# Attention's steps beside a feed-forward: from slots to a count of matmuls

## The chip, the cores and the metric

The kernel runs on one core of a Trainium2 chip. The metric is the device time of one execution in microseconds (us). TensorE multiplies matrices into PSUM (eight banks), VectorE and ScalarE work element by element and read PSUM, GpSimd (POOL) works element by element on SBUF only, and SyncE (SP) issues most of the DMA transfers.

## The reference

Three layers follow each other. The first is attention with sink and window, on q, k, v of 2 batches, 8 heads, 768 positions and 64 channels:

```python
keep = is_sink | in_window            # 4 sink keys, window of 128
scores = np.where(keep, scale * q @ k.T, -1e9)
a = np.exp(scores - scores.max(-1)); a = a / (a.sum(-1) + 1e-09)
x = a @ v                             # as 1536 tokens x 512
```

The second is a feed-forward: `g = relu(x @ w_in) ** 2`, `y = g @ w_out`, with 512 x 2048 and 2048 x 512 weights. The third is another one of the same size on y, whose activation is a rational function of `y @ w_in`. Weights come as 64-bit floats and are converted on the chip.

## The kernel before, in words

The 1536 tokens are cut into three groups of 512. The first feed-forward runs group by group (`group(g)`, L763), each in 16 blocks f of 128 hidden channels. A block has a first product (`gemm1`, L456: four parts of three matmuls into one PSUM bank; each operand is held as a high and a low part, hence three), an activation (`act1`, L471: three ScalarE and one VectorE instruction) and, two blocks later, a second product (`gemm2a`, L482: four times two matmuls on the high part, then four on the low part). So a block is 12 + 8 + 4 = 24 matmuls of 512 columns. The last two second products of a group come after its blocks, together with the split of the next group's x into high and low parts (`split_x`, L412). In group 0 the weights are loaded and converted as well (`wconv`, L635); in group 2 those of the third layer are.

Attention is cut into 24 units of two heads and 256 queries, eight for each group. The eight of group 0 run in a prologue. The other sixteen run beside groups 0 and 1, one group ahead of their use, as generators (`att_unit`, L373). A unit goes through these steps, one for each `next`: scores on TensorE into two banks, with maximum on VectorE (L203) and exponential on ScalarE (L209); the sums, their reciprocal and the scaling (VectorE and POOL, L214 to L220); nothing; the load of its values; the transposes on TensorE (L226) with one copy on ScalarE and one on VectorE (L231); the product with the values on TensorE (L245) and a ScalarE copy of the result into `x32` (L393); and a last step that only ends it. All these steps share PSUM banks 6 and 7.

`tick` (L583) does one step of every unit that is under way, and every third tick begins a new unit. So ticks carry scores, transposes and values in turn. The ticks are emitted with raised priority. In groups 0 and 1 the order of TensorE is the order of the program; on the other engines a scheduler with a cost model sets it. When ticks are called is decided by `slot` (L783), which is called three times in a block, after the first product and its activation, between the two halves of the second product, and at the block's end:

```python
nt = PER * NUNIT[g] + PER                      # 27 ticks in a group
def slot(k):
    nonlocal pos
    first = 9 if g == 0 else -2
    while pos < min(nt, nt * (k - first) // (3 * NF - first - 2)):
        tick()
        pos += 1
```

After a group's blocks, a loop calls further ticks until the units of the next group are done (L822).

Of the kernel before, what the change touches and what calls it, by code (L numbers as in the profile page):

```python
# [27 lines left out]
NF = DFF // P  # L28
# [9 lines left out]
NORM_POOL = (0,)  # L38
YEVAC_ACT = (0, 1)
PINNED = (0, 1)  # L40
NUNIT = (8, 8)
NCONV = 7
SCB = ((2, 3), (6, 7))
PER = 3
# [3 lines left out]
LAG = 2  # L48
# [207 lines left out]
class Fast:  # L256
# [116 lines left out]
    def att_unit(self, u, raws, alt):  # L373

        x = Unit(self, u, raws, alt)
        x.scores([self.att_bank() for _ in range(2)])
        for i, k in x.blocks:
            x.maximum(i, k)
            x.exponential(i, k)
        yield  # L380
        x.sum()
        for i, k in x.blocks:
            x.scale(i, k)
        for _ in range(ST_T):
            yield
        x.vv = self.att_load_v(u, 0)
        yield
        for k in range(2):
            x.transpose(k, self.att_bank())
            x.copy(k)  # L390
        yield
        x.values(self.att_bank())
        self.nc.scalar.copy(self.x32[u[0]][:, u[1], x.xs], x.ob[:, : x.n])  # L393
        yield

    def fill(self, b, n):
        z = self.zero.unsqueeze(1).to_broadcast([P, 4, P])
# [58 lines left out]
    def gemm1(self, which, f, xhi, xlo, n):  # L456
        h = self.h_bank()
        for c in range(NC):
            self.gemm1_part(which, f, c, (xhi, xlo), n, h)
        return h  # L460

    def gemm1_part(self, which, f, c, x, n, h):
        nc = self.nc
# [15 lines left out]
        nc.vector.tensor_tensor(glo, r, ghi.bitcast(F32), op=ALU.subtract)  # L479
        return ghi, glo  # L480

    def gemm2a(self, f, gg, n, acc, between):  # L482
        nc = self.nc
        ghi, glo = gg
        whi, wlo = self.w[(0, f, 1)]
        for m in range(NC):
            ms = slice(m * P, (m + 1) * P)
            nc.tensor.matmul(acc[m], whi[:, ms], ghi, start=(f == 0), stop=False)  # L488
            nc.tensor.matmul(acc[m], wlo[:, ms], ghi, start=False, stop=False)  # L489
        if between:  # L490
            between()
        for m in range(NC):
            ms = slice(m * P, (m + 1) * P)
            nc.tensor.matmul(acc[m], whi[:, ms], glo, start=False, stop=(f == NF - 1))  # L494


    def act2(self, h):
# [32 lines left out]
    def run(self, ctx):  # L530
# [46 lines left out]
        n0 = sum(1 for u in us if u[0] == 0)  # L577
        done = 0
# [4 lines left out]
        def tick():  # L583
            with ExitStack() as c:
                if urgent:
                    c.enter_context(tc.high_priority(offset=HP))
                tick_()
            self.va_hist.append((self.lastV, self.lastA))

        def tick_():  # L590
            nonlocal done, tick_no, ui
            if tick_no % PER == 0 and loaded:
                u, raws = loaded.pop(0)
                g = u[0]
                if g not in self.x32 and g > 0:
                    self.new_x32(g)
                a = self.att_unit(u, raws, 0)
                ui += 1
                next(a)
                new = True  # L600
            else:
                new = False
            for b in list(active)[::-1]:
                if next(b, "end") == "end":
                    active.remove(b)
                    done += 1
            if new:
                active.append(a)
                if not loaded:
                    prefetch()  # L610
            tick_no += 1
# [60 lines left out]
        with tc.manual_schedule(engines={E.Activation, E.DVE}):  # L672
# [43 lines left out]
            done = n0  # L716
# [4 lines left out]
        urgent = True  # L721
        acc, gs, ys, ysp = None, {}, {}, {}

        def second(which, g, f, between=None):
            nonlocal acc
            if f == 0:
                acc = [self.bank(k)[:, : GN[g] if which == 0 else 512] for k in range(4)]
            gg = gs.pop((which, g, f))
            if which == 0:
                n = GN[g]  # L730
                self.gemm2a(f, gg, n, acc, between)
                if f == NF - 1:
                    k = 0 if g == NG - 1 else g
                    y = self.yp.tile([P, self.yw[k]], F32, tag=f"y{k}", name="y")
                    y = y[:, : NC * n].rearrange("p (m n) -> p m n", m=NC)
                    for m in range(NC):
                        (A.copy if m % 2 == 0 or g in YEVAC_ACT else V.tensor_copy)(y[:, m], acc[m])
                    ys[g] = y
            else:
                self.gemm2b(f, gg, acc)  # L740
                if f == NF - 1:
                    for t in range(TG2 // P):
                        if g == NT2 - 1:
                            if t == 0:
                                ot = self.xp.tile([P, 4, DM], F32, tag="xhi", name="ot")
                            o = ot[:, t]
                        else:
                            o = self.stage.tile([P, DM], F32, tag="wt", name="o", bufs=2)
                        r0 = g * TG2 + t * P
                        dst = self.io["out"][r0 : r0 + P, :]  # L750
                        if g == NT2 - 1 and t == TG2 // P - 1:
                            A.copy(o[:, : DM // 2], acc[t][:, : DM // 2])
                            nc.scalar.dma_start(dst[:, : DM // 2], o[:, : DM // 2])
                            V.tensor_copy(o[:, DM // 2 :], acc[t][:, DM // 2 :])
                            nc.sync.dma_start(dst[:, DM // 2 :], o[:, DM // 2 :])
                        else:
                            (A.copy if t % 2 == 0 else V.tensor_copy)(o, acc[t])
                            nc.sync.dma_start(dst, o)

        gdone = [sum(1 for u in us if u[0] <= g) for g in range(NG)]  # L760
        sp, pos, nt = None, 0, 0

        def group(g):  # L763
            nonlocal sp, acc, pos, nt
            n = GN[g]
            last = g == NG - 1
            if last:
                assert done == len(us)
                sa.close()
                sp = ExitStack()  # L770
                self.ysp = mk(sp, "ysp", 1, "right")
                self.cp = self.ysp
                self.yx = self.yp.tile([P, self.yw[2]], F32, tag="y2", name="yx")
                self.flag()
                self.coefficients()
                wload(1, 3)
                nt = 0
            else:
                nt = PER * NUNIT[g] + PER
            self.att_banks = [6, 7]  # L780
            pos = 0

            def slot(k):  # L783
                nonlocal pos
                first = 9 if g == 0 else -2
                while pos < min(nt, nt * (k - first) // (3 * NF - first - 2)):
                    tick()
                    pos += 1

            for f in range(NF):  # L790
                if (g, f) == (0, 12):
                    self.hint((mybir.EngineType.SP, self.lastD))
                if g == 0 and f < HEAD:
                    h = hb[f]
                elif g == 0 and f == HEAD:
                    h = self.bank(6)
                    for c in range(NC):
                        self.gemm1_part(0, f, c, self.x[0], n, h)
                else:
                    h = self.gemm1(0, f, *self.x[g], n)  # L800
                gs[(0, g, f)] = self.act1(h, n)
                if g == 0 and f + 4 < NF:
                    wconv(0, f + 4, 0)
                if last and f > 0:
                    wconv(1, f - 1, 0)
                slot(3 * f + 1)
                if f >= LAG:
                    second(0, g, f - LAG, lambda: slot(3 * f + 2))
                else:
                    slot(3 * f + 2)  # L810
                if g == 0 and f + 1 < NF:
                    wconv(0, f + 1, 1)
                if last:
                    if f >= 3:
                        wconv(1, f - 3, 1)
                    if f in (4, 6, 8, 10):
                        with ExitStack() as cc:
                            cc.enter_context(tc.issue_after(self.lastX.ins))
                            self.split_y(0, (f - 4) // 2, ys, ysp)
                slot(3 * f + 3)  # L820
            if not last:
                while done < gdone[g + 1]:  # L822
                    tick()
                self.new_x(g + 1)
                for c in range(NC):
                    self.split_x(g + 1, c)
            else:
                wconv(1, NF - 1, 0)
            for f in range(NF - LAG, NF):
                second(0, g, f)  # L830
# [265 lines left out]
```

## Time and profile before

| | us |
|---|---|
| median of 3 runs | 633.92 (631.86 to 634.03) |
| profiled execution | 631.83 |
| its span, first to last instruction | 630.0 |
| TensorE busy | 609.5 (97%) |
| VectorE busy | 416.7 (66%) |
| ScalarE busy | 407.1 (65%) |
| GpSimd busy | 116.8 (19%) |
| mean granted TensorE clock | 0.995 |

Group 0's blocks begin at about 48 us, group 1's at about 160, group 2's at 273, the third layer's at about 365. In the rows PE is TensorE, DVE is VectorE, ACT is ScalarE. A matmul's end is modelled, so of two matmuls in a row the shown durations overlap; the distance between their starts is the time that one takes. A row that merges several instructions has their number after the x.

### The profile page before, as it was taken

How to read it: one execution, taken by the hardware profiler on the slowest of the kernel's cores; microseconds unless marked ns; L12 is line 12 of the kernel's file. 1: busy time of each engine (PE TensorE's matmuls, PEld its weight loads, DVE VectorE, ACT ScalarE, POOL GpSimd, SP SyncE). 2: the span in 40 equal slices, each digit the busy share in tenths (PEclk: the TensorE clock that was granted, in tenths of full speed). 3: DMA queues.
4: the chain of work that ended last, by engine and by line, in shares of the span. 5: the costliest groups of instructions: out<-in, count | busy, mean ns of one | idle time of the engine just before them, and what ended most of it. 6: DMA issues, size and time to landing. Idle time of an engine off the chain costs nothing.

```text
span 630.0 us, 9425 instructions
## 1 busy us (share of the span) xinstructions
PE 609.5 (97%) x3465; PEld 485.9 (77%) x3465; DVE 416.7 (66%) x832; ACT 407.1 (65%) x838; POOL 116.8 (19%) x119
## 2 busy tenths in 40 slices
PE   7889999999899999999999999999999999999996
PEld 3557777777677778888888888888888888888885
DVE  5987777454342232155666469988999897877783
ACT  4878988665554353276777567766686676766663
POOL 2220101010010000030000013234354332222221
PEclk9999999999999999999999999999999999999999
DMA  8846686434121200005555300000010000100002
GB/s 293 298 145 206 215 273 211 163 110 150 56 73 54 82 29 1 2 34 165 181 191 199 134 1 0 2 0 1 2 55 12 0 2 1 68 0 1 0 2 70
DMA packets 19347, 54.80 MB, mean 87 GB/s; under 512 B 2528, under 2 KB 3808, under 8 KB 19296
## 3 DMA queue, kind: packets, MB, share of 16 engines
q1 hardware_dynamic: 19008, 54.01, 25.7%
q8 instruction: 29, 0.48, 0.3%
q14 instruction: 22, 0.18, 0.1%
q10 hardware_dynamic: 288, 0.13, 0.1%
HBM read 50.99 MB, written 3.15 MB: 86 GB/s over the span
## 4 chain that ended last, share of the span: by engine, by line
PE 90%; DVE 4%; ACT 3%; DMA 1%; issue 1%; SPq 0%; DVEq 0%
PE b L467 14%; PE b L468 14%; PE b L469 14%; PE b L525 7%; PE b L527 7%; PE b L526 7%; PE b L488 7%; PE b L494 7%; PE b L489 7%; PE b L245 3%; PE b L189 2%; PE b L226 2%; DVE p L203 1%; ACT p L209 1%; DVE wt L135 1%; DMA nsw<-nsw 1%
## 5 line engine op out<-in xcount | busy, mean ns | idle before, releaser
L468 PE MATMUL b<-xlo,whi 128*128 128x512 f32 x256 | 100.3, 392 | 3.6 <-DVE xlo L253 2.5
L467 PE MATMUL b<-xhi,whi 128*128 128x512 f32 x256 | 101.8, 398 | 1.4 <-ACT xhi L249 1.4
L469 PE MATMUL b<-xhi,wlo 128*128 128x512 f32 x256 | 99.7, 390 | 0.0
L516 POOL TENSOR_TENSOR glo<-t,ghi 128x512 fp32r<-128x512 f32 x34 | 49.7, 1463 | 231.9 <-ACT ghi L515 205.3
L488 PE MATMUL b<-ghi,whi 128*128 128x512 f32 x192 | 76.4, 398 | 0.0
L479 DVE TENSOR_TENSOR glo<-b,ghi 128x512 fp32r<-128x512 f32 x48 | 33.2, 691 | 63.5 <-ACT b L478 63.3
L489 PE MATMUL b<-ghi,wlo 128*128 128x512 f32 x192 | 74.9, 390 | 0.0
L526 PE MATMUL b<-wlo,ghi 128*128 128x512 f32 x192 | 74.7, 389 | 0.0
L525 PE MATMUL b<-whi,ghi 128*128 128x512 f32 x192 | 74.5, 389 | 0.0
L527 PE MATMUL b<-whi,glo 128*128 128x512 f32 x192 | 66.9, 389 | 0.0
L220 POOL TENSOR_SCALAR p<-p,sums 128x224 f32<-128x224 f32 (+1 forms) x48 | 28.2, 598 | 206.8 <-DVE sums L215 179.8
L209 ACT ACTIVATE p<-p,mn 128x224 f32<-128x224 f32 (+1 forms) x96 | 43.9, 458 | 32.4 <-DVE mn L203 32.4
L450 DVE TENSOR_TENSOR wlo<-wt,whi 128x512 fp32r<-128x512 f32 x64 | 44.1, 689 | 28.9 <-ACT whi L447 28.7
L476 ACT ACTIVATE b<-b 128x512 f32<-128x512 f32 x48 | 28.4, 592 | 48.4 <-PE b L469 48.4
L447 ACT CAST whi<-wt 128x512 fp32r<-128x512 f32 x64 | 39.6, 619 | 30.5 <-PE b L468 21.9
L468 PEld LDWEIGHTS b<-xlo,whi 128*128 128x128 f32 x256 | 48.1, 188 | 14.3 <-DVE xlo L253 4.9
L467 PEld LDWEIGHTS b<-xhi,whi 128*128 128x128 f32 x256 | 48.1, 188 | 13.4 <-issue 1.7
L469 PEld LDWEIGHTS b<-xhi,wlo 128*128 128x128 f32 x256 | 48.0, 188 | 10.2
L494 PE MATMUL b<-glo,whi 128*128 128x512 f32 x192 | 53.1, 398 | 0.0
L130 ACT CAST top<-st 128x512 f16<-128x512 bf16 x64 | 49.7, 777 | 2.3 <-issue 1.5
L467 PE MATMUL b<-yhi,whi 128*128 128x512 f32 x128 | 49.8, 389 | 0.0
L468 PE MATMUL b<-ylo,whi 128*128 128x512 f32 x128 | 49.8, 389 | 0.0
(128 smaller groups left out, 1208.4 us busy)
## 6 DMA issues: line engine op xcount, KB each, us to landing
st<-w SPq DMA_DIRECT2D x64, 512.0 KB, 3.5
vv<-att SPq DMA_DIRECT2D x12, 448.0 KB, 3.4
raw<-att SPq DMA_DIRECT2D x12, 352.0 KB, 3.0
out<-o SPq DMA_DIRECT2D x8, 256.0 KB, 2.0
raw<-att SPq DMA_DIRECT2D x6, 272.0 KB, 4.0
vv<-att SPq DMA_DIRECT2D x6, 256.0 KB, 3.8
raw_e<-att SPq DMA_DIRECT2D x4, 352.0 KB, 5.4
vb<-att SPq DMA_DIRECT2D x4, 256.0 KB, 4.6
```

The lines of the kernel that those rows point to most:

```text
L130: nc.scalar.copy(top.bitcast(F16).rearrange("p (n w) -> p n w", w=2)[:, :, 1], head)
L209: self.f.lastA = self.nc.scalar.activation(p, p, AF.Exp, scale=-1.0, bias=self.mn[i, k], accum_out=self.sums[:, j : j + 1])
L467: nc.tensor.matmul(h[:, :n], whi[:, cs], xhi[:, c, :n], start=(c == 0), stop=False)
L468: nc.tensor.matmul(h[:, :n], whi[:, cs], xlo[:, c, :n], start=False, stop=False)
L469: nc.tensor.matmul(h[:, :n], wlo[:, cs], xhi[:, c, :n], start=False, stop=(c == NC - 1))
L488: nc.tensor.matmul(acc[m], whi[:, ms], ghi, start=(f == 0), stop=False)
L489: nc.tensor.matmul(acc[m], wlo[:, ms], ghi, start=False, stop=False)
L494: nc.tensor.matmul(acc[m], whi[:, ms], glo, start=False, stop=(f == NF - 1))
L516: self.lastL = nc.gpsimd.tensor_tensor(glo, t3, ghi.bitcast(F32), op=ALU.subtract)
L525: nc.tensor.matmul(acc[t], ghi[:, ts_], whi, start=(f == 0), stop=False)
L526: nc.tensor.matmul(acc[t], ghi[:, ts_], wlo, start=False, stop=False)
L527: self.lastM = nc.tensor.matmul(acc[t], glo[:, ts_], whi, start=False, stop=(f == NF - 1))
```

## The change

Slots, their number of ticks and the loop at the group's end go. Instead, `point(n)` is called inside the products, after n matmuls, and counts them; `due` is a list of 51 counts, and each time the count reaches the next one a tick is called. The counts are 40 to 336 in 26 equal steps, then 336 to 720 in 24. Group 0 counts 336 matmuls to the end of its blocks (the first products of blocks 0 and 1 are not counted), and 720 is the end of group 1's blocks. A unit ends with its values and copy instead of one tick later, and `x32` of a group is allocated at the first copy into it, not at the first scores. The units of group 2 begin before group 0 has ended, and an assertion replaces the loop.

```diff
-NUNIT = (8, 8)
+PACE = (40, 336, 720)
...
         x.values(self.att_bank())
+        if u[0] not in self.x32:
+            self.new_x32(u[0])
         self.nc.scalar.copy(self.x32[u[0]][:, u[1], x.xs], x.ob[:, : x.n])
-        yield
...
         for c in range(NC):
             self.gemm1_part(which, f, c, (xhi, xlo), n, h)
+            self.point(3)
         return h
+
+    def point(self, n):
+
+        self.count += n
+        while self.due and self.count >= self.due[0]:
+            self.due.pop(0)
+            self.tick()
...
             nc.tensor.matmul(acc[m], whi[:, ms], ghi, start=(f == 0), stop=False)
             nc.tensor.matmul(acc[m], wlo[:, ms], ghi, start=False, stop=False)
-        if between:
-            between()
+            self.point(2)
         for m in range(NC):
             ms = slice(m * P, (m + 1) * P)
             nc.tensor.matmul(acc[m], whi[:, ms], glo, start=False, stop=(f == NF - 1))
+            self.point(1)
...
-                g = u[0]
-                if g not in self.x32 and g > 0:
-                    self.new_x32(g)
...
+        na, a0, a1, a2 = PER * n0 + 2, *PACE
+        self.due = [a0 + (a1 - a0) * i / na for i in range(na)] + [a1 + (a2 - a1) * i / (na - 2) for i in range(na - 1)]
+        self.count = 0
...
-                slot(3 * f + 1)
                 if f >= LAG:
-                    second(0, g, f - LAG, lambda: slot(3 * f + 2))
-                else:
-                    slot(3 * f + 2)
+                    second(0, g, f - LAG)
...
-                slot(3 * f + 3)
             if not last:
-                while done < gdone[g + 1]:
-                    tick()
+                assert done == gdone[g + 1], (g, done)
```

## Rows read from the trace of the kernel before

**Rows 1.** Stretches of groups 0 and 1: busy us of each engine, TensorE's clock, DMA.

```profile
48.00:160.00 112.00, 109.54 (x748) 83.24 (x749) 73.55 (x197) 83.14 (x196) 11.53 (x18) 1.00 0.56 186
160.00:273.30 113.30, 111.40 (x768) 88.33 (x767) 34.43 (x109) 51.79 (x130) 8.49 (x16) 1.00 0.13 41
```

**Rows 2.** TensorE's waits: total us, times, longest.

```profile
PE b L245 <- ACT pT L231: 3.7, 6, 1.0
...
PE b L226 <- DVE mn L203: 1.6, 2, 1.0
...
PE b L245 <- DVE pT L231: 1.1, 2, 0.9
```

**Rows 3.** TensorE in order of time, group 1, undisturbed: start, us, what, [idle].

```profile
186.60 1.03 PE L226 MATMUL b<-ident,p 128*128 128x128 f32 x8
187.39 1.17 PE L494 MATMUL b<-glo,whi 128*128 128x512 f32 x4
188.39 0.39 PE L467 MATMUL b<-xhi,whi 128*128 128x512 f32 x1
...
190.89 0.39 PE L469 MATMUL b<-xhi,wlo 128*128 128x512 f32 x1
191.21 1.14 PE L245 MATMUL b<-pT,vv 128*64 128x64 f32 x28
192.27 0.50 PE L488 MATMUL b<-ghi,whi 128*128 128x512 f32 x1
```

**Rows 4.** TensorE in order of time, the disturbed places.

```profile
79.25 0.99 PE L189 MATMUL b<-raw 64*64 64x224 f32 x16
...
83.18 0.52 PE L226 MATMUL b<-ident,p 128*128 128x128 f32 x3 [0.57 <-DVE mn L203]
...
105.87 1.18 PE L494 MATMUL b<-glo,whi 128*128 128x512 f32 x4
107.35 1.13 PE L245 MATMUL b<-pT,vv 128*64 128x192 f32 x16 [0.30 <-ACT pT L231]
...
137.30 1.17 PE L494 MATMUL b<-glo,whi 128*128 128x512 f32 x4
138.48 0.33 PE L245 MATMUL b<-pT,vv 128*64 128x64 f32 x2
139.73 1.13 PE L245 MATMUL b<-pT,vv 128*64 128x64 f32 x26 [0.92 <-DVE pT L231]
...
165.10 1.03 PE L226 MATMUL b<-ident,p 128*128 128x128 f32 x8
167.04 1.14 PE L245 MATMUL b<-pT,vv 128*64 128x64 f32 x28 [0.90 <-ACT pT L231]
...
171.05 0.99 PE L189 MATMUL b<-raw 64*64 64x224 f32 x16
173.03 1.25 PE L226 MATMUL b<-ident,p 128*128 128x128 f32 x8 [1.00 <-DVE mn L203]
```

**Rows 5.** TensorE in order of time: group 1's last values, group 2's beginning.

```profile
253.07 1.14 PE L245 MATMUL b<-pT,vv 128*64 128x64 f32 x28
...
273.33 0.27 PE L908 MATMUL b<-ident,mnmax 128*1 128x128 f32 x1
```

**Rows 6.** ScalarE in order of time, end of group 1.

```profile
254.25 0.37 ACT L393 COPY x<-b 128x256 f32<-128x256 f32 x1 [1.85 <-PE b L245]
...
268.59 2.18 ACT L415 CAST xhi<-x 128x512 fp32r<-128x512 f32 x4
270.66 2.19 ACT L889 CAST yhi<-y 128x512 fp32r<-128x512 f32 x4
```

**Rows 7.** DMA issues: how many, KB each, median us to landing.

```profile
vv<-att SPq DMA_DIRECT2D x12, 448.0 KB, 3.4
```

**Rows 8.** VectorE in order of time, before the wait at 139.73.

```profile
137.35 0.17 DVE L214 TENSOR_SCALAR sums<-sums 128x4 f32<-128x4 f32 x1 [0.85 <-ACT p L209]
...
139.00 0.68 DVE L231 COPY pT<-b 128x512 f32<-128x512 f32 x1
```

More of the change, by code (lines that the diff above doesn't have):

```diff
@@ L480, in act1, with gemm2a @@
         return ghi, glo
-    def gemm2a(self, f, gg, n, acc, between):
+    def gemm2a(self, f, gg, n, acc):
         nc = self.nc
@@ L722, in run, with second @@
         acc, gs, ys, ysp = None, {}, {}, {}
-        def second(which, g, f, between=None):
+        def second(which, g, f):
             nonlocal acc
@@ L730, in second @@
                 n = GN[g]
-                self.gemm2a(f, gg, n, acc, between)
+                self.gemm2a(f, gg, n, acc)
                 if f == NF - 1:
@@ L760, in run @@
         gdone = [sum(1 for u in us if u[0] <= g) for g in range(NG)]
-        sp, pos, nt = None, 0, 0
+        sp = None
+        self.tick = tick
+        na, a0, a1, a2 = PER * n0 + 2, *PACE
+        self.due = [a0 + (a1 - a0) * i / na for i in range(na)] + [a1 + (a2 - a1) * i / (na - 2) for i in range(na - 1)]
+        self.count = 0
         def group(g):
-            nonlocal sp, acc, pos, nt
+            nonlocal sp, acc
             n = GN[g]
@@ L776, in group @@
                 wload(1, 3)
-                nt = 0
-            else:
[L779 to L786, printed above, removed]
-                    tick()
-                    pos += 1
             for f in range(NF):
@@ L798, in group @@
                         self.gemm1_part(0, f, c, self.x[0], n, h)
+                        self.point(3)
                 else:
@@ L805, in group @@
                     wconv(1, f - 1, 0)
-                slot(3 * f + 1)
                 if f >= LAG:
-                    second(0, g, f - LAG, lambda: slot(3 * f + 2))
-                else:
-                    slot(3 * f + 2)
+                    second(0, g, f - LAG)
                 if g == 0 and f + 1 < NF:
@@ L819, in group @@
                             self.split_y(0, (f - 4) // 2, ys, ysp)
-                slot(3 * f + 3)
             if not last:
-                while done < gdone[g + 1]:
-                    tick()
+                assert done == gdone[g + 1], (g, done)
                 self.new_x(g + 1)
```

## The prediction

> **What bounds the kernel now.** I read the stretches first [rows 1]. In both feed-forward groups that carry attention, TensorE is the bound: of 112.0 us in group 0 it is busy 109.54, of 113.3 us in group 1 it is busy 111.40, at a granted clock of 1.00. VectorE (73.55 and 34.43) and ScalarE (83.14 and 51.79) are not full in either. So all idle time that any new order could win there is 2.46 + 1.90 = 4.36 us as the profile counts idle, plus what its modelled matmul ends hide.
>
> The second view is TensorE's waits [rows 2]: nearly all of what it waits for after the prologue is attention's own small steps, not weights or feed-forward data. Values (L245) wait for the copies of the transposed probabilities (L231), and transposes (L226) wait for the row maximum (L203), which frees their PSUM bank. The third view is the order of time on TensorE, an undisturbed stretch against the disturbed ones [rows 3, 4]. In the undisturbed one the feed-forward matmul has a pitch of (190.89 - 188.39) / 11 = 0.227 us, a transpose step takes 187.39 - 186.60 = 0.79, the four-matmul end of a second product 188.39 - 187.39 = 1.00, a values step 192.27 - 191.21 = 1.06 [rows 3]. In the disturbed places the reader is to see that two steps of attention stand four feed-forward matmuls apart, or none, so that the second comes before the other engines have answered the first: 107.35 (four matmuls after its transposes), 138.48 and 139.73 (four), 167.04 (none), 173.03 (none); 83.18 is eight matmuls after the scores [rows 4].
>
> **Where the old spacing comes from.** Ticks are given out at three slots per feed-forward block, of 12, 8 and 4 matmuls, 27 ticks to a group, so rounding sets them. Counted through the slot formula, the distances in group 0 are mostly 8, 12, 16 or 20 matmuls, with six of 4; at the start of group 1, where the first two blocks have no second product, tick 28 (transposes) and 29 (values) fall together, and 30 (scores) and 31 (transposes) too. The attention of group 1 then ends at 253.07 + 1.06 us while the group runs to 273.33 [rows 5].
>
> **The change, step by step.**
>
> 1. *Spacing.* The due counts are 40 + 296 i / 26 in group 0 and 336 + 16 i after it. Run through the points (3 after each part of the first product, 2 and 1 in the second), distances in group 0 are 9 to 14 matmuls, mean 11.4, and in group 1 15 to 17. In time: 9 to 14 times 0.227 = 2.0 to 3.2 us, then 3.4 to 3.9. Each tick still carries exactly one TensorE step (scores, transposes, values in turn), so the number of steps and matmuls is unchanged: 16 units, 48 steps.
>
> 2. *What each wait needs.* Transposes to values with nothing between: 167.04 - 165.10 = 1.94 from start, so 1.15 beyond the 0.79. With ScalarE and VectorE busy: 139.73 - 137.30 = 2.43 after the transposes' end, the longest I found. Scores to transposes: at 173.03 the wait was over 1.98 after the scores began (171.05), about 1.0 after they ended; at 83.18 it was 3.93 after they began, the longest. The new distances cover the ordinary case everywhere (2.0 against 1.0 to 1.15), and the two longest to within about 0.5 us. So the listed waits go.
>
> 3. *The sum.* By the idle column: 0.57 + 0.30 + 0.92 + 0.90 + 1.00 = 3.69 us [rows 4]. By starts, which see what modelled ends hide: at 105.87, 1.48 against 1.00, 0.48; at 137.30, 1.18 against 1.00, 0.18; at 138.48, 1.25 less two of 28 matmuls of 1.06 us (0.08), 1.17; at 165.10, 1.94 against 0.79, 1.15; at 83.18, 0.57 plus the same 0.25 that the column misses at 167.04, 0.82; at 173.03, 1.00. Sum 4.80. I take the second, since start times are observed.
>  The Trainium skill, in Perfetto Trace Analysis, section Tensor Engine Instruction (MATMUL, LD_WEIGHTS), says that a matmul's end is computed from its size and not observed. The 0.90 of idle against 1.15 between starts agrees with that; by the column alone the gain would be 3.7.
>
> 4. *New breaks.* Two pairs of steps that stood side by side now have feed-forward matmuls between them. A break costs what a step adds at its edges: the four matmuls before it take 1.00 instead of 4 x 0.227 = 0.91, so 0.09, and I count the same after it; two pairs, four edges, 0.36. I take -0.3. That a break now falls inside a first product instead of at its end I cost at nothing: another bank is written, and no row shows an edge dearer in one place than in another; bounds: -0.1 to 0.1 on each of some 25 steps, so -2.5 to 2.5.
>
> 5. *Group 0's end.* The drain ticks go. The last values of group 0 move from just after block 15's first product to the end of block 13's second product, 12 matmuls later, and the split of x follows. The cover is 24 matmuls of the last two second products, 5.4 us, and one scores step. The work under it is copy 0.37, cast 2.18 for four [rows 6], and a VectorE subtraction of a size whose copy takes 0.68 [rows 8]: about 3.3. Nothing is exposed. If that cover were gone it would cost up to 3.3.
>
> 6. *Group 1's end.* The last values move from 253.07 to the very end of the block loop [rows 5]. The same 5.4 us cover the same 3.3 [rows 6]. ScalarE is the next late one: at 270.66 it takes up casts of y, four in 2.19, which if they came first would make the path 1.06 + 0.37 + 2.19 + 2.18 + 0.68 = 6.5 against 1.06 + 5.4. That is even, so I take 0 with 0 to 1 as bound.
>
> 7. *DMAs and queues.* A unit still issues one load of scores' operands and one of values, on SP. Values are loaded two ticks ahead at the latest, 22 matmuls and two steps, some 6.7 us, against 3.4 to landing [rows 7]: hidden. POOL's two scalings per unit move with their tick and POOL is busy 11.53 of 112 [rows 1]. Allocating x32 later issues nothing; the dropped seventh tick of a unit issued nothing either.
>
> Sum: -4.8 + 0.3 = -4.5 us. The profiled execution took 631.83 us (span 630.0, 1.8 around it): 627.3. It lies 2.1 below the median of the runs shown, 633.92 (631.86 to 634.03). A new median should carry the same offset, so I forecast 633.92 - 4.5 = 629.4 us.
>
> **Rivals.**
>
> *A. Group 0's waits form again elsewhere.* For it: VectorE's queue had a copy behind work it had to wait for [rows 8], and at 11 matmuls the two longest needs are met only just. Against: only three of its waits are listed, all at 4 or 8 matmuls. Then only group 1's start is won, 1.15 + 1.00 = 2.15: 631.8 us, no change.
>
> *B. The queue order of VectorE decides, and it is slower.* In a tick the newer unit's sums are emitted ahead of the older unit's copy. At 137.35 VectorE sat 0.85 us for the exponentials and the copy came at 139.00 [rows 8], with TensorE waiting until 139.73. The evenly spaced order puts every sum one tick after its scores, with weight conversion and first-product activations between. If every unit of group 0 paid as this one did, 0.18 + 1.17 = 1.35 each, nine units cost 12.2; less the 4.8 won, 7.4 slower: 641.3 us. It decides from the point where the copy ends more than 2.5 us (11 matmuls) after the transposes; 2.43 was the longest, so it needs ScalarE to be later than ever seen.
>  The Trainium skill, in PSUM — Partial Sum Buffer, section Engine vs sequencer instructions, says that VectorE's and ScalarE's queues are strictly first in, first out and that matmuls start in program order. The trace agrees: the copy stood behind the wait of 0.85 us, and the matmuls behind the values. By that rule this rival is possible at every tick.
>
> *C. It doesn't do what it says at the groups' ends.* The last unit finishes so late that the split holds up the next group's first product, by up to 3.3 at group 1's end (step 5's price without cover). Then 4.5 - 3.3 = 1.2 is left: 632.7 us, no change. Against: 24 matmuls stand between.
>
> **How the numbers follow.** No change means within 0.5%, 3.2 us, about what a measurement of this kernel can tell. Forecast 0.68, A 0.17, C 0.09, B 0.06. The forecast's own range is 3.5 to 6.5 us won, 627.4 to 630.4; of the offset between executions of the same program (2.1) I add a good half below: 626.2. Above, A and most of C come in: 632.8. Faster 0.69 (the forecast, and a little of A), same 0.24, slower 0.07 (B and the edges of step 4).
>
> **What would show it.** Right: the waits of values on copies and of transposes on maxima all but gone from TensorE's list between 55 and 270 us; idle of the two stretches below 1.5 us; the last values near 265 us; group 2 beginning some 4.5 us earlier, and everything from there to the end shifted by that amount and no more. Step 2 is wrong if waits on L231 remain in group 0; step 4 if the idle goes but the stretch stays as long; steps 5 and 6 if the first product's first matmul of a group waits for its split. The prediction as a whole is wrong if the start of group 2 moves by less than 3.2 us.

## The result and the profile after

The changed kernel takes 627.19 us in the median of four runs (626.72 to 627.80), the kernel before 632.97 beside it (631.86 to 634.03): ratio 0.9904 with a 95% interval of 0.9879 to 0.9928. Run again beside some of the experiments, it took 626.55 against 632.84, ratio 0.9905 (0.9877 to 0.9933). Forecast were 629.4 us and a gain of 4.5; the medians moved by 5.8.

A total mixes in the prologue, which differs between executions of one program (last section). For causes I use one stretch of the profiled execution that leaves it out: from the first second-product matmul of block 0 to the last first-product matmul of the third layer, the same matmuls in every kernel. Its two ends, for the kernel before (start, us, what):

```profile
53.07 0.39 PE L488 MATMUL b<-ghi,whi 128*128 128x512 f32 x1
...
613.28 0.39 PE L469 MATMUL b<-yhi,wlo 128*128 128x512 f32 x1
```

and for the changed one:

```profile
53.40 0.39 PE L497 MATMUL b<-ghi,whi 128*128 128x512 f32 x1
...
608.42 0.39 PE L478 MATMUL b<-yhi,wlo 128*128 128x512 f32 x1
```

560.21 us became 555.02: 5.2 us won. A second profile of the changed kernel (after_again) has 554.94; every other kernel has one profile. (The two profiled executions differ by only 631.83 - 627.80 = 4.0: the changed one began the stretch 0.33 later, and its end behind the stretch was 0.8 longer.)

The stretches of groups 0 and 1 after, with the columns of [rows 1] (us, busy us and count of PE, PEld, DVE, ACT, POOL, granted clock, DMA share, GB/s):

```profile
48.00:160.00 112.00, 110.57 (x760) 85.14 (x761) 72.04 (x191) 82.29 (x194) 10.76 (x18) 1.00 0.57 187
158.00:271.24 113.24, 113.24 (x789) 89.46 (x788) 36.20 (x116) 54.52 (x134) 10.47 (x18) 1.00 0.14 41
```

Idle time fell from 2.46 to 1.43 us in group 0's stretch, and from 1.90 to nothing in group 1's. Of TensorE's waits after the prologue, the list from 55 to 272 us, one is left. It stands against the five waits, 3.69 us, that the prediction listed [rows 2, 4] (total us, times, longest):

```profile
PE b L226 <- DVE mn L203: 0.6, 1, 0.6
```

TensorE in order of time after, at the one wait, at the start of group 1, and where group 1 ends:

```profile
80.03 0.99 PE L189 MATMUL b<-raw 64*64 64x224 f32 x16
...
83.35 0.49 PE L226 MATMUL b<-ident,p 128*128 128x128 f32 x3
84.40 0.52 PE L226 MATMUL b<-ident,p 128*128 128x128 f32 x3 [0.56 <-DVE mn L203]
...
158.81 0.99 PE L189 MATMUL b<-raw 64*64 64x224 f32 x16
159.72 0.50 PE L497 MATMUL b<-ghi,whi 128*128 128x512 f32 x1
...
161.68 1.03 PE L226 MATMUL b<-ident,p 128*128 128x128 f32 x8
...
166.05 1.14 PE L245 MATMUL b<-pT,vv 128*64 128x64 f32 x28
...
264.51 1.14 PE L245 MATMUL b<-pT,vv 128*64 128x64 f32 x28
...
271.20 0.48 PE L476 MATMUL b<-xhi,whi 128*128 128x512 f32 x1
```

At the start of group 1 the transposes begin 1.96 us after the newer unit's scores have ended (159.72 to 161.68), the values 3.58 us after the transposes' 0.79 (to 166.05), and neither waits. (Scores and the transposes behind them belong to two units, which share the PSUM banks; transposes and values belong to one.) The wait at 84.40 is the old one at 83.18 [rows 4], on the same unit.

### The profile page after: what moved, and what is told of

Read it like the earlier page. It is cut to its first block, busy times and chain, and to the rows that moved or that the text cites. A ratio compares the mean times of both kernels' runs of the same rounds, so it can differ in the third digit from the quotient of the medians.

```text
span 625.9 us, 9412 instructions
## 1 busy us (share of the span) xinstructions
PE 608.2 (97%) x3465; PEld 485.6 (78%) x3465; DVE 412.8 (66%) x832; ACT 407.7 (65%) x838; POOL 112.9 (18%) x119
## 4 chain that ended last, share of the span: by engine, by line
PE 89%; DVE 5%; ACT 3%; issue 1%; DMA 1%; DVEq 0%
PE b L476 14%; PE b L477 14%; PE b L478 13%; PE b L534 7%; PE b L536 7%; PE b L535 7%; PE b L497 7%; PE b L502 6%; PE b L498 6%; PE b L245 3%; PE b L189 2%; PE b L226 2%; DVE p L203 1%; ACT p L209 1%; DVE wt L135 1%
## 5 line engine op out<-in xcount | busy, mean ns | idle before, releaser
L525 POOL TENSOR_TENSOR glo<-t,ghi 128x512 fp32r<-128x512 f32 x34 | 48.4, 1424 | 228.9 <-ACT ghi L524 117.1
L536 PE MATMUL b<-whi,glo 128*128 128x512 f32 x192 | 68.5, 389 | 0.0
L478 PE MATMUL b<-yhi,wlo 128*128 128x512 f32 x128 | 49.8, 389 | 0.0
```

The costliest lines, as they stand in the source:

```text
L478: nc.tensor.matmul(h[:, :n], wlo[:, cs], xhi[:, c, :n], start=False, stop=(c == NC - 1))
L525: self.lastL = nc.gpsimd.tensor_tensor(glo, t3, ghi.bitcast(F32), op=ALU.subtract)
L536: self.lastM = nc.tensor.matmul(acc[t], glo[:, ts_], whi, start=False, stop=(f == NF - 1))
```

## The experiments

The theory, D in the texts quoted, is that the distance in matmuls between attention's steps decides. All edits are against the changed kernel.

| kernel | median us | ratio to the kernel before (95%) | stretch us |
|---|---|---|---|
| before | 632.97 | | 560.21 |
| after | 627.19 | 0.9904 (0.9879 to 0.9928) | 555.02 |
| after_again | 626.55 | 0.9905 (0.9877 to 0.9933) | 554.94 |
| e1_old_grid | 634.43 | 1.0025 (1.0012 to 1.0037) | 560.73 |
| e2_old_group0 | 632.23 | 0.9982 (0.9967 to 0.9996) | 558.58 |
| e3_old_group1 | 630.46 | 0.9966 (0.9952 to 0.9980) | 558.11 |
| e4_values_at_once | 649.55 | 1.0260 (1.0232 to 1.0288) | 577.46 |
| e5_values_after_4 | 635.08 | 1.0029 (1.0011 to 1.0047) | 562.21 |
| e6_group1_dense | 627.58 | 0.9909 (0.9882 to 0.9936) | 555.52 |
| e7_wider_answers | 629.34 | 0.9945 (0.9927 to 0.9963) | 556.83 |
| e8_counts_at_slots | 629.67 | 0.9949 (0.9930 to 0.9968) | 557.66 |
| e9_wider_copy_first | 627.99 | 0.9932 (0.9908 to 0.9955) | 555.40 |
| e10_after_4_copy_first | 633.04 | 1.0006 (0.9988 to 1.0024) | 560.50 |
| e11_copy_first | 628.32 | 0.9933 (0.9916 to 0.9951) | 555.71 |

**The old distances, in the new code (e1, e2, e3).** The steps' counts of the kernel before are put into the new list, for both groups, for group 0 alone, for group 1 alone.

```diff
+ old0 = [44, 48, 68, 72, 84, 96, 108, 116, 132, 140, 156, 164, 168, 188, 192, 204, 216, 228, 240, 252, 260, 276, 284, 288, 308, 312, 324, 336]
+ old1 = [372, 372, 384, 384, 396, 408, 428, 444, 452, 468, 480, 500, 516, 524, 540, 552, 572, 576, 596, 612, 624, 644, 648]
+ self.due = old0 + old1                # e1
+ self.due = old0 + self.due[28:]       # e2
+ self.due = self.due[:28] + old1       # e3
```

> The changed kernel with every other edit kept (points inside the products, no drain ticks, no seventh step, later x32), but its list of due counts set to those at which the old slots gave the ticks (44, 48, 68, ... 336, then 372, 372, 384, 384, ... 648). Theory D (distance: the time was lost where two steps of attention stand 0 to 8 matmuls apart): the whole gain goes, within 0.5% of the kernel before (631 to 635 us beside a before of 633), TensorE waits on the L231 copies and the L203 maxima for about 4 us again. Rival E (the other edits: run-on across the group's end, no drain, one step less, later x32): at least half of the gain of 5.8 us stays, 630 us or less.

> The changed kernel with the old due counts in group 0 alone, even ones in group 1. Theory D: group 0's waits come back, 0.82 + 0.48 + 0.18 + 1.17 = 2.65 us and up to 0.5 of smaller ones, so 2.6 to 3.2 slower than the changed kernel and about 2.5 faster than before. Rival S (what helps is that group 1's attention now reaches to its end): nothing comes back, equal to the changed kernel.

> The changed kernel with even due counts in group 0 and the old ones in group 1 (two pairs of steps at one count, attention over 72 matmuls before the end). Theory D: the two waits at group 1's start come back, 1.15 + 1.00 = 2.15 us, less two breaks saved (0.36): 1.8 slower than the changed kernel, about 3.5 to 4 faster than before; the later distances of group 1 (4 to 20) cost nothing, since VectorE and ScalarE are idle there. Rival S: nearly the whole gain goes.

With both old lists the whole gain is gone: the stretch is 560.73, within 0.6 us of before, so D holds and the rest of the new code is worth about nothing. The old waits are back at their old places, the one of 1.00 for maxima too; in e1 the values with nothing before them:

```profile
166.62 1.03 PE L226 MATMUL b<-ident,p 128*128 128x128 f32 x8
...
168.55 1.14 PE L245 MATMUL b<-pT,vv 128*64 128x64 f32 x28 [0.90 <-ACT pT L231]
```

e1's median is 1.6 us above that of the kernel before beside it (632.82) although its stretch is only 0.5 longer. Its profiled execution shows a granted clock of 0.83 from 8 to 28 us, where before and after show 0.91, and the mean granted clock of its runs is 0.991 in the median, against 0.993 for the kernel before beside it, so I do not read the edit from that total.

Group 0's old list costs 3.6 us (expected 2.6 to 3.2): besides its waits it brings back a scores step cut in two, by feed-forward matmuls in its middle, for some 0.7 us, which the expectation left out (step 3 below). Group 1's costs 3.1 (expected 1.8). They add up to 6.7 against e1's 5.7. The difference lies in e3, where one of group 1's waits is twice as long as in e1. TensorE first, then ScalarE:

```profile
162.60 1.03 PE L226 MATMUL b<-ident,p 128*128 128x128 f32 x8
...
165.57 1.14 PE L245 MATMUL b<-pT,vv 128*64 128x64 f32 x28 [1.93 <-ACT pT L231]
```

```profile
162.50 2.01 ACT L743 COPY y<-b 128x512 f32<-128x512 f32 x4
...
164.92 0.60 ACT L231 COPY pT<-b 128x512 f32<-128x512 f32 x1
```

With the new group 0 in front, the transposes come as ScalarE begins to empty the four banks of y, and the copy waits behind 2.01 us of that. So the price of a short distance depends on what happens to be in the answering queue just then.

**Values close behind their transposes (e4, e5).** Only the third step of each unit is moved.

```diff
+ self.due = [self.due[i - 1] if i % 3 == 2 else d for i, d in enumerate(self.due)]      # e4
+ self.due = [self.due[i - 1] + 4 if i % 3 == 2 else d for i, d in enumerate(self.due)]  # e5
```

> The changed kernel with each unit's values given at the count of its transposes, so that no feed-forward matmul stands between them, in all 16 units. Theory D: each values step waits for its copies. In group 1 some 1.15 us (as at 167.04 before), in group 0 1.2 to 2.7 after the transposes' end (what the copies took in the changed kernel's trace), so 9 x 2.0 + 7 x 1.15 = 26, less 16 breaks of 0.2: 23 us slower than the changed kernel, about 650. If distance were only worth what the page calls idle, 0.9 each, it would be 14 - 3 = 11 slower.

> The changed kernel with each values step 2 to 6 matmuls (mostly 3 or 4) behind its transposes in all 16 units. Theory D with the loads: in group 1, where VectorE and ScalarE are idle half of the time, the copies end 0.73 us after the transposes, and 3 matmuls are 0.68: nothing or 0.2 each. In group 0 they ended 1.2 to 2.7 after them, so each of nine units waits 0.3 to 1.8, together 6 to 10 us: 633 to 638, stretch 561 to 566. Rival T (a fixed number of matmuls decides, as 4 did for three of the kernel before's waits): group 1 pays as much per unit as group 0.

e4's stretch grew by 22.4 us (expected 23), e5's by 7.2 (expected 6 to 10). Some 2.8 of e4's 22.4 are not waiting but a lower clock (last section), so the waits cost about 19.6, and that 22.4 lies so near to 23 is in part luck; 11, the price by the idle column, is out either way. The first unit of group 0 in e4, and an ordinary one of group 1:

```profile
72.55 1.03 PE L226 MATMUL b<-ident,p 128*128 128x128 f32 x8
...
76.29 1.98 PE L245 MATMUL b<-pT,vv 128*64 128x64 f32 x28 [2.71 <-ACT pT L231]
...
192.89 1.03 PE L226 MATMUL b<-ident,p 128*128 128x128 f32 x8
194.17 0.33 PE L245 MATMUL b<-pT,vv 128*64 128x64 f32 x2 [0.24 <-ACT pT L231]
194.71 1.13 PE L245 MATMUL b<-pT,vv 128*64 128x64 f32 x26 [0.22 <-DVE pT L231]
```

In this unit of group 1 the first copy comes 0.5 us beyond the step (192.89 + 0.79 to 194.17), and both are there 1.0 beyond it (194.71). In group 0, with weights still being converted, values waited until 2.95 beyond it (72.55 + 0.79 to 76.29). Three or four matmuls (e5) cover the first and nearly the second: seven of group 1's eight values steps have no wait in e5's list and cost 0.15 us each by starts. Its first unit waits, as in e3, for a copy behind the emptying of y (in e4 until 2.33 us beyond its transposes), and so does the first of group 0, whose transposes begin at 74.35:

```profile
78.08 1.14 PE L245 MATMUL b<-pT,vv 128*64 128x64 f32 x28 [1.78 <-ACT pT L231]
...
171.67 1.14 PE L245 MATMUL b<-pT,vv 128*64 128x64 f32 x28 [1.39 <-ACT pT L231]
```

So the ten or so matmuls of the new spacing are needed in group 0 and at the start of group 1, and are far more than the rest of group 1 needs. What rival T expects of e5 did not come.

**An earlier end of group 1 (e6).** `PACE = (40, 336, 528)` instead of 720 packs group 1's steps into the first half of it, 6 to 9 matmuls apart.

> The changed kernel with group 1's due counts from 336 to 528 instead of 720, so its steps stand 6 to 9 matmuls apart (1.4 to 2.0 us) and its attention ends some 45 us before the group. Theory D: 1.4 to 2.0 us cover group 1's needs (0.73 for the copies, 1.5 to 1.9 for the maxima) but for a few tenths: equal to the changed kernel within 0.2%. Rival S (attention should reach to the group's end): slower by 2 us or more.

The stretch grew by 0.5 us. Ending late gives nothing that could be seen, so rival S falls. One scores step took 1.64 (163.24 to 164.88) instead of 0.91, which is more than the whole of it:

```profile
163.24 1.72 PE L189 MATMUL b<-raw 64*64 64x224 f32 x16
164.88 0.50 PE L476 MATMUL b<-xhi,whi 128*128 128x512 f32 x1
```

No matmul stands between the values before it (from 162.17) and this step. Its fifth matmul began at 163.98, when ScalarE's copy of the values' result had ended at 163.93. That is a third pair with a distance to keep, from values to the next unit's scores; the prediction lists only two.

**More room for the maxima (e7).** The wait that is left is for maxima, so scores come one count earlier, transposes 1.5 and values 1 later, in group 0.

```diff
+ shift = (-1, 1.5, 1)
+ self.due = [d + shift[i % 3] if i < 26 else d for i, d in enumerate(self.due)]
```

> The changed kernel with group 0's due counts shifted by -1, 1.5 and 1 for scores, transposes and values: 12 to 15 matmuls from scores to transposes instead of 10 to 14, 10 to 12 from transposes to values, 8 to 11 from values to scores. Theory D: the one wait of TensorE that the changed kernel kept, 0.56 us of a transposes step for maxima, gets smaller or goes and none comes in its place: stretch 0.3 to 0.8 us shorter, too little to see in the total (within 0.2%).

This failed: the wait for the maxima went (0.75), but the stretch is 1.8 us longer. A values step takes 1.43 us more (88.57 below), a scores step cut in two 0.7, another scores step 0.4 (both are shown with e9 and e11). TensorE, then VectorE in e7:

```profile
83.85 0.82 PE L226 MATMUL b<-ident,p 128*128 128x128 f32 x6
...
88.57 0.89 PE L245 MATMUL b<-pT,vv 128*64 128x192 f32 x14 [0.89 <-DVE pT L231]
```

```profile
85.47 0.17 DVE L214 TENSOR_SCALAR sums<-sums 128x4 f32<-128x4 f32 x1 [0.84 <-ACT p L209]
...
85.90 0.78 DVE L220 TENSOR_SCALAR p<-p,sums 128x224 f32<-128x224 f32 x2
...
87.20 0.85 DVE L135 SCALAR_TENSOR_TENSOR wt<-st,top 128x512 int32<-128x512 int32 x1
87.97 0.54 DVE L231 COPY pT<-b 128x384 f32<-128x384 f32 x1
```

VectorE sat 0.84 us for the newer unit's exponentials, then did that unit's sums and scalings and two conversions, and only then the older unit's copy, which ended at 88.51, 3.8 us after the modelled end of the transposes (84.67). That is rival B's mechanism, once.

**Steps only at three places of a block (e8).** The new counts, but points only after the first product (12), between the halves of the second (8) and after it (4).

> The changed kernel's due counts, but looked at only at the three old places (after a first product, between the halves of a second, at its end), so that distances in group 0 are 8 to 16 with two of 4, and 12 to 20 in group 1; no step stands inside a first product or a half of a second. Theory D: group 1 as in the changed kernel; group 0 pays where 4 or 8 matmuls follow, six to nine places at 0.2 to 1.0: stretch 557 to 560 against 555.0. Rival F (steps inside the products are what is cheaper, whatever the distance): the stretch is longer in group 1 too, by 0.1 or more at each step. Rival G (steps inside the products are dearer): shorter in group 1.

557.66, as expected (557 to 560): the counts alone give half the gain, the finer points the other half. By starts, its steps are 3.2 us too long in all, against 0.76 in the changed kernel; the largest wait, with scores from 81.04:

```profile
84.05 1.14 PE L226 MATMUL b<-ident,p 128*128 128x128 f32 x6 [0.90 <-DVE mn L203]
```

Scores and transposes are close again, with only the four matmuls of a second product's end between them. Rivals F and G fall: in the middle of group 1 the twelve matmuls between transposes and values take 182.63 - 179.72 = 2.91 us in e8, 0.19 more than 12 x 0.227, and the fifteen in the changed kernel 0.18 more than theirs (208.74 - 205.15 = 3.59), though of the two only the changed kernel has steps inside products.

**The copy before the sums (e9, e10, e11, and after_again).** The older unit's step goes first in a tick, and VectorE's sums are held until its copy is issued. e9 is this with e7's counts, e10 with e5's, e11 with the changed kernel's own.

```diff
- for b in list(active)[::-1]:
+ for b in list(active):
...
- x.sum()
+ with ExitStack() as c:
+     if self.lastC is not None:
+         c.enter_context(self.tc.issue_after(self.lastC.ins))
+     x.sum()
...
+ self.lastC = x.copied          # VectorE's copy, after it is emitted
```

> The kernel with the wider answers (12 to 15 matmuls from scores to transposes), which had one new wait of 0.89 us idle at a values step, where VectorE did the newer unit's sums and scalings and two weight conversions before the copy. Here the order of emission in a tick is older unit first, and the sums are queued behind the older unit's copy on VectorE. Theory Q (the order on VectorE's queue made the new wait): it goes, stretch 556.8 down to 554.5 to 555.6. Rival: the copies are late for ScalarE's sake, and the stretch stays above 556.3.

> The kernel with values 2 to 6 matmuls behind their transposes (stretch 562.2), with the same order as the kernel beside it: sums behind the older unit's copy on VectorE. Theory Q: VectorE's share of group 0's waits goes, some 1 to 2.5 us; ScalarE's copy still stands behind exponentials and weight casts, so 559.7 to 561.2. If distance alone counted, whatever the queue holds, it would stay at 562.2 +- 0.3.

> The changed kernel with sums behind the older unit's copy on VectorE and nothing else. No values step waited for VectorE there, so theory Q gives the changed kernel's stretch, 555.0 +- 0.4, and its time within 0.2%; the copies in group 0 should end sooner after their transposes than the 2.7 us seen (below 2.0).

> The changed kernel itself, beside the others on one chip: 0.988 to 0.993 of the kernel before. In the profiles so far, from the first second product to the last first product of the third layer, the kernel before took 560.2 us and the changed one 555.0; the rest of the difference between executions lies in the prologue, where the granted clock stood at its lower level for 3 to 10 us. Theory P (the prologue's clock is luck of the execution): that stretch is again 555.0 +- 0.3, whatever the total.

e9 takes e7's wait away, and its stretch falls from 556.83 to 555.40 (expected 554.5 to 555.6). VectorE at the same place, the copy ahead of the sums:

```profile
86.00 0.55 DVE L231 COPY pT<-b 128x384 f32<-128x384 f32 x1
86.47 0.16 DVE L214 TENSOR_SCALAR sums<-sums 128x4 f32<-128x4 f32 x1
```

From 55 to 272 us e9 shows no TensorE wait at all, yet it is 0.4 us longer than the changed kernel. The same holds for e11 (555.71, expected 555.0 within 0.4: missed by 0.3), which keeps the wait for maxima. Both have one thing that the changed kernel lacks, here in e11:

```profile
158.99 0.59 PE L189 MATMUL b<-raw 64*64 64x224 f32 x4
159.51 0.50 PE L481 MATMUL b<-xlo,whi 128*128 128x512 f32 x1
...
160.18 0.97 PE L189 MATMUL b<-raw 64*64 64x224 f32 x12
161.08 0.50 PE L501 MATMUL b<-ghi,whi 128*128 128x512 f32 x1
```

A scores step cut in two by two feed-forward matmuls: 161.08 - 158.99 = 2.09 us, where an uncut step (0.91, from 158.81 to 159.72 in the changed kernel) and two matmuls (0.45) take 1.36. So 0.73 goes there, and that answers for all of e11's 0.7. In e11 VectorE's copies did end sooner (0.73 us after the first unit's transposes, 1.56 in the changed kernel, both from the modelled end), but ScalarE's did not: the longest is 2.68, where below 2.0 was expected.

For e9 the balance (won: 0.76 of wait; lost: 0.73) leaves 0.4, and that is the third pair again. ScalarE, then TensorE:

```profile
90.08 0.38 ACT L399 COPY x<-b 128x256 f32<-128x256 f32 x1
```

```profile
90.12 1.20 PE L189 MATMUL b<-raw 64*64 64x128 f32 x16
```

This scores step takes 1.14 us (to 91.26), the same one in the changed kernel 0.75 (91.16 to 91.91). The copy of the older unit's result ends at 90.46, and the step's fifth matmul begins at 90.51. The counts of e7 and e9 had brought scores closer to the values before them (2.03 us behind their end here, 2.72 in the changed kernel). Uncut, e9 might come out ahead; that wasn't tried. None of these beats the changed kernel.

e10 landed at 560.50 (expected 559.7 to 561.2): of e5's 7.2 us the new order was worth 1.7. Of that 0.45 came at group 1's first values (their wait for ScalarE's copy fell from 1.39 to 0.94), so not all of it is VectorE's queue. Most of the rest is ScalarE's half of the copy, which stands behind two weight conversions, with values waiting 1.79 us for it until 76.96:

```profile
75.20 0.60 ACT L452 CAST whi<-wt 128x512 fp32r<-128x512 f32 x1
75.70 0.76 ACT L130 CAST top<-st 128x512 f16<-128x512 bf16 x1
76.34 0.57 ACT L231 COPY pT<-b 128x512 f32<-128x512 f32 x1
```

## Why the prediction was right, by its own steps

**Steps 1 and 2, spacing and what each wait needs.** Right as a mechanism: distance decides (e1 undoes the gain, e4 and e5 buy the waits back). The distances came as counted inside the groups, but not where group 0 ends: from 159.72 to 161.68 there are eight matmuls, by the counts about sixteen. Step 2's last sentence, "so the listed waits go", failed for one of them. It had the longest need as 3.93 us from the beginning of the scores and a new distance that met it only to within 0.5; in the changed kernel that distance is 83.35 - 80.03 = 3.32, and the need had grown to 84.40 - 80.03 = 4.37. VectorE's first maximum of this unit in the kernel before, then its maxima in the changed one:

```profile
81.10 0.39 DVE L203 CUSTOM_DVE_ANT_0 p<-b,m 128x224 f32<-128x224 f32 x1
```

```profile
82.32 0.39 DVE L203 CUSTOM_DVE_ANT_0 p<-b,m 128x224 f32<-128x224 f32 x1
...
83.86 0.38 DVE L203 CUSTOM_DVE_ANT_0 p<-b,m 128x224 f32<-128x224 f32 x1
```

In both kernels VectorE has a weight conversion in the middle of the maxima. What grew is the time until it begins on them: 81.10 - 79.25 = 1.85 us after the scores began, now 82.32 - 80.03 = 2.29, in both right behind another weight conversion, which now stands later against the scores. So what failed in step 2 is the need, taken as a constant of the kernel: it changes with what stands in the same queue.

**Step 3, the sum.** 4.80 was forecast by starts. The same count over the kernel before, with every place where a step took over 0.27 us too long, gives 5.40, and a scores step cut in two (four at 155.13, twelve at 157.93) 0.52 more: 5.92. After, 0.76 is left. So 5.16 was won by this count, and the stretch shows 5.19. By terms:

| term | forecast | measured |
|---|---|---|
| transposes at 83.18, wait for maxima | 0.82 | 0.01 (0.77 before, 0.76 after) |
| values at 107.35 | 0.48 | 0.57 |
| values at 138.48 and 139.73 | 1.35 | 1.52 |
| transposes at 147.54, no idle listed in the profile | not summed | 0.32 |
| scores cut in two at group 0's end | not summed | 0.52 |
| values at 167.04 | 1.15 | 1.15 |
| transposes at 173.03 | 1.00 | 1.07 |

A term that was to go and stayed (0.82), and two that no idle time pointed at (0.84), nearly cancel: that 4.5 lies so near to 5.2 is in part luck. That starts see more than the idle column was right: the column would have made it 3.7.

**Step 4, new breaks.** Forecast to cost 0.3, and by the rows they do. Where the kernel before had nothing between two steps, the changed one has eight matmuls that take 161.68 - 159.72 = 1.96 us, 0.14 more than 8 x 0.227, and fifteen that take 166.05 - 161.68 - 0.79 = 3.58, 0.17 more. The count of step 3 is too rough to show these 0.31: it leaves out such edges, those of the cut step among them, so its 5.16 lies closer to 5.19 than it should. The step's other half, that a break inside a product costs no more than one at its end, held (e8). What does cost is a break inside attention's step: 0.73 in e11 and, counted in the same way (158.84 - 155.13, less 0.91 and nine matmuls), 0.76 in the kernel before.

**Steps 5 and 6, the groups' ends.** Right. ScalarE after group 1's last values in the changed kernel, against [rows 6]:

```profile
265.69 0.37 ACT L395 COPY x<-b 128x256 f32<-128x256 f32 x1 [0.66 <-PE b L245]
266.10 0.62 ACT L416 CAST xhi<-x 128x512 fp32r<-128x512 f32 x1
266.63 2.18 ACT L882 CAST yhi<-y 128x512 fp32r<-128x512 f32 x4
```

Three of the four casts were done beforehand, the last came ahead of the casts of y, and group 2's first product began at 271.20 with no idle before it. Rival C is out, and so is the even race that step 6 feared. The margin at group 0's end is not wide, though: in e4 and e5 group 1's first products waited for their split, 0.77 and 0.36 us at the longest.

**Step 7, loads.** No wait on a load stands in TensorE's list after 55 us.

**The marker that misled.** "The prediction as a whole is wrong if the start of group 2 moves by less than 3.2 us": the first matmul of group 2 moved from 273.33 [rows 5] to 271.17, by 2.2. But in the kernel before a whole second product of group 1 still ran behind it, from 276.21 to the next first product at 278.93. Its last four matmuls:

```profile
278.02 1.07 PE L494 MATMUL b<-glo,whi 128*128 128x512 f32 x4
```

In the changed kernel those twelve matmuls (2.72 us) ran before the mark, and the stretch began 0.33 later: 2.2 + 2.7 + 0.3 = 5.2. The order across the group's end isn't pinned, so the marker was badly chosen, not the sum wrong.

**The rivals.** A is out: one wait of group 0 stayed, none formed anew. B's mechanism is real: in e7 VectorE's copy, behind the newer unit's sums, came 3.8 us after the transposes. In the changed kernel the latest copy, after the transposes at 72.30, ended 2.71 us after these (at 76.04), beyond B's 2.5 and only 0.18 us ahead of the values at 76.22. That one was ScalarE's, behind a weight conversion; VectorE's had ended 1.56 after. The Trainium skill, in PSUM — Partial Sum Buffer, section Engine vs sequencer instructions, calls VectorE's queue strictly first in, first out; e7 (copy behind the sums, a wait of 0.89) and e9 (copy first, none) agree. But in e7 it hit one unit, not nine, and in the changed kernel none: it took shifted distances (e5, e7) to pay for it.

**The total.** 629.4 was forecast, 627.19 measured. Of the 2.2 us, 0.7 is the gain (5.2, not 4.5), 0.95 the median of before, which came to 632.97 instead of 633.92, and 0.6 is left, which is no more than the spread of the totals between executions.

## What to carry to other kernels

When short steps of one chain are woven into a long run of matmuls, place them by the distance that the answering engines need, and look for that distance where those engines are busiest: here 1.0 us beyond the transposes in most of one group, 2.3 at its start and up to 2.95 in the other. Look at every pair that shares a PSUM bank: values and the next scores were such a pair too (e6, e9). Sum such a change by the starts of the steps, not by the idle column, and look for a step that is cut in two, which shows no idle at all. For a mark of success take two instructions that enclose the same work in both kernels.

## What the runs showed of the hardware

The granted clock differs between executions of one program, and most of the spread of the totals goes with it: six runs of the changed kernel took 626.25 to 626.65 us at a mean granted clock of 0.997 (four of them) and 629.08 and 628.64 at 0.991 and 0.992. In the profiles the lower level stands in the prologue. From 8 to 28 us, in the changed kernel and in e2:

```profile
8.00:28.00 20.00, 15.23 (x185) 10.33 (x179) 16.34 (x72) 14.70 (x51) 4.52 (x8) 0.91 0.97 342
```

```profile
8.00:28.00 20.00, 14.93 (x149) 10.09 (x142) 14.24 (x62) 12.97 (x43) 4.51 (x8) 0.74 0.90 322
```

A difference of 1 us between two kernels' totals can be this alone. In e4 the clock fell in the middle of the kernel as well, during the wait of 2.71 us before 76.29: 0.57 of full speed from 75 to 83 us, most of it at the lower of the two levels, 1.2 GHz.

```profile
75.00:83.00 8.00, 6.71 (x41) 5.61 (x42) 6.24 (x12) 6.28 (x12) 0.53 (x2) 0.57 0.71 238
```

By starts, the values step there took 1.91 us (76.29 to 78.20) instead of 1.07, and the next 24 feed-forward matmuls 7.63 (to 85.83) instead of the 5.67 that 24 took at full clock (117.20 to 122.87): 2.8 us, about as much as the wait itself.
